# A gated long convolution with a routed feed-forward on one core: first filter block on ScalarE's DMA queue, keys and values as two pieces, another order of issue

## Chip, cores and metric

One core of a Trainium2 chip. The metric is the device time of one execution in microseconds (us), the median of several runs. A core has five engines with one instruction stream each: TensorE (PE in the profile, its weight loads PEld), VectorE (DVE), ScalarE (ACT), GpSimd (POOL) and SyncE (SP). Each works through its stream in order; an instruction that waits holds everything behind it on its engine. DMAs are issued by SP, by ACT or by POOL, and issuing one takes time on the issuing engine (SPq, ACTq, POOLq in the rows).

## What is computed

The input is 2048 tokens of 640 channels. The reference, cut to what matters:

```python
mod = (silu(c) @ w_mod)                 # six vectors sa, ca, ga, sb, cb, gb
h = layernorm(x) * (1 + ca) + sa
x = x + ga * A(h, k, v, shift_k, ssm_k, ssm_D)
h = layernorm(x) * (1 + cb) + sb
x = x + gb * B(h, w_r, w_gate, w_up, w_down)

def A(q, k, v, ...):
    kv = shift(k) * v                   # 4-tap causal convolution of k, per channel
    y  = irfft(rfft(kv) * rfft(ssm_k))  # causal convolution of length 2048, per channel
    return q * (y + kv * ssm_D)

def B(x, ...):                          # only the 8 tokens with the largest r = x @ w_r
    y = (silu(xs @ w_gate) * (xs @ w_up)) @ w_down * sigmoid(r[idx])
    return x + scatter_add(y at idx)
```

## The kernel before

The 640 channels are five blocks of 128, and each block goes through the same steps. The long convolution is a discrete Fourier transform in two steps, with the length 2048 split as 16 times 128, so that both steps are matrix products. Names of steps stand in the table `ORDER`, with the block's number behind them:

- `LK b` loads keys `kT` and values `vT` of block b, transposed by the DMA (`load_kv`, L129 and L130, on SP's queue). `LG b` loads the filter block `gA` (`load_g`, L140). `LX` loads a quarter of x into `xq` (L658).
- `C b` (`t_C`): PE forms the 4-tap convolution of `kT` with four diagonal matrices `dg` (`DIAG b`, L309) in two halves of 1024 tokens; each half is multiplied by `vT` into `kvT` (L80; in the starred form ACT copies the half first, L77, and DVE multiplies after it, L78), and written to DRAM as `kvd` (L373). `kvT` has a single buffer. `LXA b` reads `kvd` back in another layout as `xA` (L145).
- `G b` and `X b` (`stage_A`): the first step of the transform, of the filter and of the signal, four PSUM tiles each, copied out as `A`. Ahead of `G b` the skip weights `Dt` are added to the filter (L353).
- `BG b` and `BX b` (`stage_B`): the second step with the tables `FT`, four tiles each, copied out as `HX`. `P b` multiplies the two spectra on DVE (L406, L407, L409, L410).
- `BT b`: the first step back, with the tables `IT`; its tiles `U` go to DRAM (`UW`) and come back as `uA` (`LU`). `AT b` is the last step, multiplied by the normalised rows `h`, and `AA b` adds the result to `xq`.
- `Sx` are the statistics of the first layernorm (L664), `H` builds `h` from them and from the modulation vectors (`LW` loads, `MOD` computes). `R`, `GR`, `COL` and `GB` prepare the second layernorm and the scores.
- `T` is, in 11 parts, the choice of the 8 tokens, their feed-forward and the scattered addition to the output; `N`, `BS`, `BL` and `F` are the normalisation and the output rows of all tokens (16 halves `F`: a product L735 and a sum L737, then a DMA to the output). `WG` and `WD` load the feed-forward's weights.

Every copy out of PSUM goes to ACT or, where the name in `ORDER` ends in a star, to DVE (the class `Evac`). There are four PSUM tiles for these results, used in turn. PE, DVE and ACT all work in the order in which `ORDER` names the steps; `:n` means n parts of a step. Nothing else sets the order.

At the start, `SC`, `SA`, `SB`, `SD`, `SE`, `SG`, `SH` and `TC` make constants: POOL counts and compares (`trig` for the tables, `ident`, the mask `early` from `erow` and `ecol`, `arow`, `irow`, `onesb`), `TAB` turns `trig` into `FT` by sines on ACT, `RA` makes the matrix of `stage_A`, and `WU` runs 13 matmuls on zeros. `SG` sets `Dt` to zero on POOL (L236) and then loads the skip weights into it on SP's queue (L240). In `SA` ACT issues three small loads: `shk_bf` (the 4 taps, L201), `cT_bf` (L202) and `wr_c` (L203). `silu_c`, which the modulation starts from, needs `cT_bf`.

Of the kernel before, what the change touches and what calls it, by code (L numbers as in the profile page):

```python
# [9 lines left out]
P = 128  # L10
BF = mybir.dt.bfloat16
# [6 lines left out]
S_TOK = 2048  # L18
# [14 lines left out]


ORDER = """
SH SB0 LG0 SA TAB0 SC SE SG WU TAB0 RA SB1 SD TAB1 RAT RA LK0 G0 DIAG0 LG1 LX G0* LK1 C0 TAB1 DIAG1 G0* IT* G0
C0 BG0 LX TC BG0 G1 LXA0 Sx G1* Sx IT:2 C1:2 G1* LG2 G1 LXA1 BG0 BG0* LW BG1 Sx BG1* X0:3 X0* BG1 LK2 LX BX0 Sx
BX0:3 RAT Sx:2 DIAG3 Sx P0 BG1 X1* X1 G2 Sx DIAG2 LX X1 P0 X1 P0 LW C2:2 MOD G2 BX1:2 P0 G2 BX1 LW LXA2 G2 Sx
BT0:4 Sx P1 BG2 Sx:2 LW Sx:4 LK3 Sx BG2 LG3 P1 MOD BX1 LW MOD OG H LW X2:4 C3*:2 BG2 LW BX2 BG2 UW0 P1 BT1 BT1*
G3:2 H DIAG4 LXA3 MOD:2 LW P1 LK4 BX2* G3 UW1 H BX2:2 P2:2 BT1 H G3 MOD UW0 MOD BT1 P2 LW X3:2 LG4 X3 BG3 H C4*  # L40
X3 C4 H BT2 BG3 P2 BX3 BG3 H BX3 P3 BX3 WG BT2 UW1 WG LXA4 H P3 BT2 WG BT2 MOD BX3 BG3 G4*:2 G4 MOD P3 UW2 G4
X4:3 X4* BG4 P3 BG4* BX4 UW2 BX4 BG4 BX4 LU0 LU2 BG4 BX4 LU1 BT3:2 H P4:4 BT3 H:3 BT3 BT4:2 UW3 BT4 UW3 UW4 BT4
AT0*:2 AA0:2 AT1* COL UW4 LU3 AT1 R0 AA1:2 AT2* GB LU4 WG AA2 WG AT2* GR R0 WG AA2 WG R1 AT3 AT3* WG:2 R1 R2
AA3:2 AT4 AA4 GR AT4* R2 AA4 BS* R3 BS* GR R4 COL WD BL* R3 BS* GR:3 R4 T WD BS T N N* N:4 F BS WG T F BL F T N
F BS F T F N F:2 N:2 F N:2 F N BS F T N F N F N F BS F T F T:4
"""


# [14 lines left out]
def _kernel_body(ctx, tc, A_q, A_k, A_v, A_shift_k, A_ssm_k, A_ssm_D,  # L63
                 B_w_r, B_w_gate, B_w_up, B_w_down, c, w_mod, out):
    nc = tc.nc
# [22 lines left out]
    ring = ctx.enter_context(tc.tile_pool(name="ring", bufs=1))  # L88
# [35 lines left out]

    def load_kv(b):
        kT = ring.tile([P, 16 + S_TOK], BF, name="kT", tag="K", bufs=5)
        vT = ring.tile([P, S_TOK], BF, name="vT", tag="K", bufs=5)
        nc.gpsimd.memset(kT[:, 0:16], 0.0)
        nc.sync.dma_start_transpose(out=kT[:, 16:16 + S_TOK], in_=k_d[:, b * P:(b + 1) * P])  # L129
        nc.sync.dma_start_transpose(out=vT[:], in_=v_d[:, b * P:(b + 1) * P])  # L130
        kTs[b], vTs[b] = kT, vT

    def rows_ap(handle_ap, b, rowlen, run):

        return bass.AP(tensor=handle_ap.tensor, offset=handle_ap.offset + b * P * rowlen,
                       ap=[[run, P], [8 * rowlen, 16], [1, run]])
# [29 lines left out]
    cT_bf = const.tile([P, NB], BF, name="cT_bf")  # L166
    wr_c = const.tile([P, NB], BF, name="wr_c")
# [26 lines left out]
    def iota(o, pat, base=0, cm=0):  # L194
        nc.gpsimd.iota(o, pattern=pat, base=base, channel_multiplier=cm, allow_small_or_imprecise_dtypes=True)
# [3 lines left out]
    def t_SA():  # L199
        with nc.allow_non_contiguous_dma(reason="tiny transposed loads"):  # L200
            nc.scalar.dma_start(out=shk_bf[:], in_=A_shift_k.rearrange("(b p) j -> p b j", p=P))  # L201
            nc.scalar.dma_start(out=cT_bf[:], in_=c.rearrange("o (t p) -> p (o t)", p=P))  # L202
            nc.scalar.dma_start(out=wr_c[:], in_=B_w_r.rearrange("(t p) -> p t", p=P))  # L203
        for i, v in enumerate((PI, -PI, -math.pi / 2, -4096.0, -0.5)):
            G.memset(bias[:, i:i + 1], v)
        nc.scalar.activation(out=junk1[:], in_=bias[:, 2:3], func=ACT.Sin)
        iota(pidx[:], [[0, 1]], cm=1)
        yield
# [501 lines left out]
    tiny = lambda name, dt=F32: small.tile([P, M], dt, name=name)  # L710
# [207 lines left out]
@with_exitstack  # L918
def kernel(
    ctx: ExitStack,  # L920
    tc: tile.TileContext,
    A_q: bass.AP,
    A_k: bass.AP,
    A_v: bass.AP,
    A_shift_k: bass.AP,
    A_ssm_k: bass.AP,
    A_ssm_D: bass.AP,
    B_x: bass.AP,
    B_w_r: bass.AP,
    B_w_gate: bass.AP,  # L930
    B_w_up: bass.AP,
    B_w_down: bass.AP,
    c: bass.AP,
    w_mod: bass.AP,
    out: bass.AP,
):
    _kernel_body(ctx, tc, A_q, A_k, A_v, A_shift_k, A_ssm_k, A_ssm_D,
                 B_w_r, B_w_gate, B_w_up, B_w_down, c, w_mod, out)
# [30 lines left out]
```

## Time and profile before

| | |
|---|---|
| median of 3 runs | 172.56 us (171.92 to 173.59) |
| the profiled execution | 171.51 us, its span 169.7 us |
| PE, DVE, ACT, POOL busy in the span | 146.4, 145.1, 136.0, 35.7 us |
| DMA | 40.71 MB, 240 GB/s on average |

Times in the rows are us from the start of the span, of one execution. In a timeline a row gives start, duration, engine, line, operation, output and input, and in brackets the idle time before it and what ended it. A row of the waits gives who waited for what: us in total, times, the longest. In the table of windows each row is a stretch with its length and then the busy time and the number of instructions on PE, PEld, DVE, ACT and POOL, the granted clock of PE (1.00 is 2.4 GHz, 0.50 is 1.2 GHz), the DMA share and GB/s. A row of the chain gives start, duration and what. A row of groups gives line, operation, shapes, count, busy us and mean ns; a row of DMA issues gives the count, the size and the us to landing.

### The profile page before, as it was taken

To read this page: it belongs to the slowest core of one execution; us is meant where nothing else is said; L and a number is where in the kernel's file an instruction comes from. 1 tells how busy PE (TensorE), PEld (TensorE's weight loads), DVE (VectorE), ACT (ScalarE), POOL (GpSimd) and SP (SyncE) were. 2 spreads that over 40 slices of the span, in tenths; PEclk is the share of its full clock that TensorE was granted. 3 is DMA by queue.
4 is the path that set the end of the run, shared out by engine and by line. 5 is a ranking of instruction groups with operands and counts; after the bars stand their busy time and mean duration, and the time that the engine had idled before them with its cause. 6 is when DMAs were issued, how large, how long until landed. Compare 5 with 4: busy or idle time off the path is not lost.

```text
span 169.7 us, 4737 instructions
## 1 busy us (share of the span) xinstructions
PE 146.4 (86%) x1983; PEld 114.3 (67%) x1983; DVE 145.1 (85%) x265; ACT 136.0 (80%) x150; POOL 35.7 (21%) x78
## 2 busy tenths in 40 slices
PE   0869998988999999999999989999899883969850
PEld 0336856887488866898589869979788761257540
DVE  3667838899999929999999999999999998979940
ACT  3979694699889999989989999999498624999700
POOL 8838900060000062970000000000000102200003
PEclk9999999999999999999999999999999997595555
DMA  6299999999999999999999999997997369665640
GB/s 120 5 177 255 243 239 296 268 281 208 342 328 278 232 171 250 265 292 186 339 232 349 277 351 301 282 321 292 278 313 242 108 194 372 175 160 190 220 159 2
DMA packets 73405, 40.71 MB, mean 240 GB/s; under 512 B 45160, under 2 KB 70184, under 8 KB 73384
## 3 DMA queue, kind: packets, MB, share of 16 engines
q1 hardware_dynamic: 69560, 38.19, 88.0%
q10 hardware_dynamic: 3744, 2.22, 4.4%
q8 instruction: 15, 0.25, 0.7%
q0 software_dynamic: 80, 0.01, 0.1%
q14 instruction: 6, 0.05, 0.1%
HBM read 24.67 MB, written 10.50 MB: 207 GB/s over the span
## 4 chain that ended last, share of the span: by engine, by line
DVE 60%; DMA 12%; PE 10%; issue 6%; SPq 4%; POOL 3%; POOLq 1%; ACT 1%; DVEq 0%; ACTq 0%
DVE T L406 6%; DVE HX L407 5%; DVE A L58 5%; DMA kvd<-kvT 4%; DVE kvT L80 3%; DMA vT<-in_A_v_dram 3%; DVE st L664 3%; DMA kT<-in_A_k_dram 3%; DVE HX L410 3%; DVE HX L409 3%; DVE HX L58 3%; DVE xq L472 3%; DVE h L679 3%; DVE h L675 3%; PE p L367 2%
## 5 line engine op out<-in xcount | busy, mean ns | idle before, releaser
L60 ACT CAST HX<-ps 128x1024 bf16<-128x1024 f32 x28 | 27.8, 1045 | 3.5 <-PE ps L390 3.5
L386 PE MATMUL ps<-A,FT 128*128 128x256 bf16 x124 | 28.4, 273 | 0.4 <-DVE kvT L80 0.3
L388 PE MATMUL ps<-A,FT 128*128 128x128 bf16 x124 | 27.2, 219 | 0.0
L390 PE MATMUL ps<-A,FT 128*128 128x128 bf16 x124 | 27.2, 219 | 0.0
L60 ACT CAST A<-ps 128x1024 bf16<-128x1024 f32 x22 | 22.4, 1067 | 3.9 <-PE ps L346 3.9
L390 PEld LDWEIGHTS <-FT 128*128 128x128 bf16 x160 | 15.6, 98 | 1.8
L60 ACT CAST U<-ps 128x1024 bf16<-128x1024 f32 x16 | 16.2, 1079 | 0.5 <-ACT A L60 0.5
L386 PEld LDWEIGHTS <-FT 128*128 128x128 bf16 x160 | 15.6, 98 | 1.4 <-DVE A L58 0.9
L388 PEld LDWEIGHTS <-FT 128*128 128x128 bf16 x160 | 15.7, 98 | 1.2 <-issue 0.7
L424 PE MATMUL ps<-IT,HX 128*128 128x256 bf16 x68 | 15.4, 273 | 0.3 <-DVE HX L410 0.3
L422 PE MATMUL ps<-IT,HX 128*128 128x256 bf16 x68 | 15.4, 272 | 0.0
L367 PEld LDWEIGHTS <-dg 128*128 128x128 bf16 x80 | 7.7, 98 | 9.1 <-DVE dg L309 0.4
L664 DVE BATCH_NORM_STATS2 st<-xq 128x6 f32<-128x320 bf16 x32 | 13.3, 478 | 0.1
L309 POOL TENSOR_SCALAR dg<-ident,shk_f 128x128 bf16<-128x128 bf16 x16 | 12.6, 804 | 3.2 <-DVE shk_f L306 3.2
L407 DVE TENSOR_TENSOR HX<-HX 128x2048 bf16<-128x2048 bf16 x10 | 12.3, 1225 | 0.3
L406 DVE TENSOR_TENSOR T<-HX 128x2048 bf16<-128x2048 bf16 x10 | 12.2, 1216 | 0.0
L60 ACT COPY xT<-ps 128x2048 bf16<-128x2048 bf16 x4 | 7.5, 1865 | 3.8 <-PE ps L527 3.1
L353 POOL TENSOR_TENSOR gA<-gA,Dt 128x16 bf16<-128x16 bf16 x4 | 3.8, 942 | 30.4 <-DMA gA<-in_A_ssm_k_dram 15.9
L60 ACT CAST A<-p 128x1024 bf16<-128x1024 f32 x9 | 9.5, 1052 | 0.7 <-PE p L346 0.6
L367 PE MATMUL p<-kT,dg 128*128 128x512 bf16 x40 | 9.5, 379 | 0.4 <-DMA kT<-in_A_k_dram 0.3
L346 PEld LDWEIGHTS <-xA 128*128 128x128 bf16 x80 | 7.7, 97 | 3.0 <-issue 1.8
L346 PEld LDWEIGHTS <-gA 128*128 128x128 bf16 x80 | 7.5, 98 | 3.2 <-DVE shk_f L306 1.7
(259 smaller groups left out, 389.4 us busy)
## 6 DMA issues: line engine op xcount, KB each, us to landing
Ud<-U SPq DMA_DIRECT2D x10, 512.0 KB, 4.5
uA<-Ud SPq DMA_DIRECT2D x10, 512.0 KB, 7.0
gA<-in_A_ssm_k_dram SPq DMA_DIRECT2D x5, 512.0 KB, 5.3
xq<-in_A_q_dram SPq DMA_DIRECT2D x4, 640.0 KB, 5.2
kvd<-kvT SPq DMA_DIRECT2D x10, 256.0 KB, 3.3
xA<-kvd SPq DMA_DIRECT2D x5, 512.0 KB, 4.8
early<-in_w_mod_dram SPq DMA_DIRECT2D x3, 800.0 KB, 7.3
wm<-in_w_mod_dram SPq DMA_DIRECT2D x6, 400.0 KB, 6.2
```

The source lines that it names most:

```text
L58: self.nc.vector.tensor_copy(out=out, in_=in_)
L60: self.nc.scalar.copy(out=out, in_=in_)
L346: nc.tensor.matmul(ps[:, bb // 2, :, (bb % 2) * 8:(bb % 2) * 8 + 8], lhsT=src[:, 4 * g4 + bb, :], rhs=RA[:].rearrange("p k c e -> p (k c) ...
L367: nc.tensor.matmul(ps[:, i, :], lhsT=diags[b][:, j, :], rhs=kT[:, n0 - j:n0 - j + 512], start=(j == 0), stop=(j == 3))
L386: nc.tensor.matmul(ps[:, i], lhsT=FT[:, 0, k2, :], rhs=A[:, 2 * k2:2 * k2 + 2, u, :], start=True, stop=False)
L388: nc.tensor.matmul(ps[:, i, 0, :], lhsT=FT[:, 1, k2, :], rhs=A[:, 2 * k2 + 1, u, :], start=False, stop=False)
L390: nc.tensor.matmul(ps[:, i, 1, :], lhsT=FT[:, 2, k2, :], rhs=A[:, 2 * k2, u, :], start=False, stop=True)
L406: V.tensor_tensor(out=T2[:], in0=X, in1=Hi, op=ALU.mult)
L407: V.tensor_tensor(out=X, in0=X, in1=Hr, op=ALU.mult)
L422: nc.tensor.matmul(ps[:, i, :], lhsT=hx[:, k2, 0, 1, :], rhs=IT[:, k2, 1:3, :].rearrange("p a b -> p (a b)"), start=True, stop=False)
L424: nc.tensor.matmul(ps[:, i, :], lhsT=hx[:, k2, 1, 1, :], rhs=IT[:, k2, 0:2, :].rearrange("p a b -> p (a b)"), start=False, stop=True)
L664: V.bn_stats(out=st1[:, m, hf, :], in_=xq[:, m, hf * 320:hf * 320 + 320])
```

## The change

Three things are edited, and with them the whole table `ORDER`.

The filter of block 0 is loaded by ACT's queue in `SA`, behind `shk_bf`; the loads of `cT_bf` and `wr_c` leave `SA` and become a step `SY`, issued by SP. `load_kv` becomes a step of two parts, so that keys and values can stand at different places of the order.

```diff
     def load_kv(b):
         kT = ring.tile([P, 16 + S_TOK], BF, name="kT", tag="K", bufs=5)
-        vT = ring.tile([P, S_TOK], BF, name="vT", tag="K", bufs=5)
         nc.gpsimd.memset(kT[:, 0:16], 0.0)
         nc.sync.dma_start_transpose(out=kT[:, 16:16 + S_TOK], in_=k_d[:, b * P:(b + 1) * P])
+        yield
+        vT = ring.tile([P, S_TOK], BF, name="vT", tag="K", bufs=5)
         nc.sync.dma_start_transpose(out=vT[:], in_=v_d[:, b * P:(b + 1) * P])
         kTs[b], vTs[b] = kT, vT
+        yield
...
             nc.scalar.dma_start(out=shk_bf[:], in_=A_shift_k.rearrange("(b p) j -> p b j", p=P))
-            nc.scalar.dma_start(out=cT_bf[:], in_=c.rearrange("o (t p) -> p (o t)", p=P))
-            nc.scalar.dma_start(out=wr_c[:], in_=B_w_r.rearrange("(t p) -> p t", p=P))
+            load_g(0, nc.scalar)
...
+    def t_SY():
+        with nc.allow_non_contiguous_dma(reason="tiny transposed loads"):
+            nc.sync.dma_start(out=cT_bf[:], in_=c.rearrange("o (t p) -> p (o t)", p=P))
+            nc.sync.dma_start(out=wr_c[:], in_=B_w_r.rearrange("(t p) -> p t", p=P))
+        yield
...
-                  LK=lambda b: once(load_kv, b), LG=lambda b: once(load_g, b), LXA=lambda b: once(load_xA, b))
+                  LK=load_kv, LG=lambda b: once(load_g, b), LXA=lambda b: once(load_xA, b))
...
-SH SB0 LG0 SA TAB0 SC SE SG WU TAB0 RA SB1 SD TAB1 RAT RA LK0 G0 DIAG0 LG1 LX G0* LK1 C0 TAB1 DIAG1 G0* IT* G0
+SC SA SD SB0 RA SG LK0:2 WU TAB0:2 SB1 SE TAB1:2 LG1 RA LX DIAG0 G0*:4 LK1 C0:2 BG0:2 DIAG1 G1* G1 LK1 BG0 LXA0
```

On POOL the constants stand in another order: ahead of the memset of `Dt` there are now `pint`, the counter `early`, `bias`, `pidx`, `ident` and the first `trig`; `arow`, `irow` and `onesb` come much later, and the mask behind the second `trig`.

The start of SP's queue, in the kernel before:

```order
L140 DMA gA<-in_A_ssm_k_dram 128x16x128
L240 DMA Dt<-in_A_ssm_D_dram 8x80x1
L129 DMA_TRANSPOSE kT<-in_A_k_dram 128x2048
L130 DMA_TRANSPOSE vT<-in_A_v_dram 128x2048
L140 DMA gA<-in_A_ssm_k_dram 128x16x128
L658 DMA xq<-in_A_q_dram 128x4x640
L129 DMA_TRANSPOSE kT<-in_A_k_dram 128x2048
L130 DMA_TRANSPOSE vT<-in_A_v_dram 128x2048
L373 DMA kvd_238<-kvT 128x1024 x2
L658 DMA xq<-in_A_q_dram 128x4x640
L145 DMA xA<-kvd_238 128x16x128
```

The same stretch now (the first `kT` and `vT` are those of block 0, the second those of block 1):

```order
L247 DMA Dt<-in_A_ssm_D_dram 8x80x1
L128 DMA_TRANSPOSE kT<-in_A_k_dram 128x2048
L131 DMA_TRANSPOSE vT<-in_A_v_dram 128x2048
L142 DMA gA<-in_A_ssm_k_dram 128x16x128
L665 DMA xq<-in_A_q_dram 128x4x640
L128 DMA_TRANSPOSE kT<-in_A_k_dram 128x2048
L380 DMA kvd_241<-kvT 128x1024 x2
L131 DMA_TRANSPOSE vT<-in_A_v_dram 128x2048
L147 DMA xA<-kvd_241 128x16x128
L665 DMA xq<-in_A_q_dram 128x4x640
```

The write of block 0's product has moved ahead of block 1's values, and its reading back ahead of the second quarter of x; the first filter block is gone from this queue.

DVE's stream around block 3's product and the first products of `P`, in the kernel before:

```order
L409 TENSOR_TENSOR HX_461<-HX_461,T2_113 128x8x128
L410 TENSOR_TENSOR HX_461<-HX_461,T2_113 128x8x128
L592 TENSOR_TENSOR modv_101<-modv_101 128x640
L593 TENSOR_TENSOR modv_101<-modv_101 128x640
L675 TENSOR_SCALAR h_929<-xq_102,rs1_120,nm1_121 128x640 x4
L78 TENSOR_TENSOR kvT_960<-kvT_960,vT_850 128x1024 x2
L406 TENSOR_TENSOR T2_114<-HX_461 128x2048
```

And now, from the first half of that product to the second:

```order
L78 TENSOR_TENSOR kvT_927<-kvT_927,vT_855 128x1024
L416 TENSOR_TENSOR HX_382<-HX_382,T2_113 128x8x128
L417 TENSOR_TENSOR HX_382<-HX_382,T2_113 128x8x128
L413 TENSOR_TENSOR T2_114<-HX_382 128x2048
L414 TENSOR_TENSOR HX_382<-HX_382 128x16x128
L599 TENSOR_TENSOR modv_101<-modv_101 128x640
L600 TENSOR_TENSOR modv_101<-modv_101 128x640
L78 TENSOR_TENSOR kvT_927<-kvT_927,vT_855 128x1024
```

The two halves stood side by side; now six other instructions stand between them. Block 4's halves stood side by side too and are nine instructions apart now, a pair L413 and L414 (L406 and L407 before) among them as here.

Copies out of PSUM are shared out a little differently: all four of `G0` are on DVE now, two of the three `IT` copies instead of one; one `HX` copy moves from DVE to ACT. In the last part DVE forms five `base` sums of 1024 elements by itself instead of four, and ACT five instead of six. In the tail the first of the two `hT` products stands behind four more halves of `F` than before, and the second one further back by one half.

## Rows read from the trace of the kernel before

**Rows 1.** Windows: three stages, from the start to the end.

```profile
0.00:26.07 26.07, 19.39 (x142) 11.59 (x143) 15.27 (x33) 19.23 (x19) 16.67 (x54) 1.00 0.92 175
...
38.39:118.27 79.88, 78.05 (x784) 64.30 (x782) 75.97 (x108) 76.16 (x88) 11.96 (x9) 1.00 1.07 279
...
140.11:169.70 29.59, 18.45 (x320) 11.49 (x320) 21.05 (x63) 17.89 (x24) 3.82 (x8) 0.59 0.56 182
```

**Rows 2.** Waits, of the engines and of SP's queue.

```profile
DVE kvT L80 <- DMA kvd<-kvT: 3.5, 1, 3.5
...
DVE nm L668 <- POOL rs L667: 3.1, 1, 3.1
...
ACT modv L576 <- PE p L570: 1.6, 1, 1.6
...
SPq L240 <- POOL Dt L236: 4.9, 1, 4.9
```

**Rows 3.** Timeline of POOL, its first 8 us.

```profile
0.85 0.34 POOL L195 IOTA arow<- 128x128 f32 x1 [0.41 <-POOLq L953]
...
1.51 1.01 POOL L195 IOTA trig<- 128x1024 f32 x1
...
3.11 0.77 POOL L195 IOTA erow<- 128x128 f32 x1
...
5.95 0.16 POOL L236 MEMSET Dt<- 128x80 bf16 x1
...
7.04 0.20 POOL masks.py:197 MEMSET ident<- 128x128 bf16 x1
...
7.99 0.15 POOL L128 MEMSET kT<- 128x16 bf16 x2
```

**Rows 4.** Timeline of SP's queue to the first read back.

```profile
6.14 0.79 SPq L240 DMA_DIRECT2D Dt<-in_A_ssm_D_dram  x1
...
14.06 4.97 SPq L129 DMA_TRANSPOSE kT<-in_A_k_dram  x1
19.07 3.13 SPq L130 DMA_TRANSPOSE vT<-in_A_v_dram  x1
...
26.00 0.37 SPq L145 DMA_DIRECT2D xA<-kvd  x1
```

**Rows 5.** The chain that ended last, its two early DMAs.

```profile
6.99 5.50 DMA kT<-in_A_k_dram
...
22.92 3.03 DMA kvd<-kvT
```

**Rows 6.** DMA issues, the reading back of the products.

```profile
xA<-kvd SPq DMA_DIRECT2D x5, 512.0 KB, 4.8
```

**Rows 7.** Timeline of DVE, three places.

```profile
10.92 0.23 DVE L353 TENSOR_TENSOR gA<-gA,Dt 128x16 bf16<-128x16 bf16 x1 [1.07 <-DMA Dt<-in_A_ssm_D_dram]
...
38.39 1.20 DVE L406 TENSOR_TENSOR T<-HX 128x2048 bf16<-128x2048 bf16 x1
...
161.35 0.20 DVE L854 TENSOR_TENSOR hT<-gs,ps 128x48 bf16<-128x48 bf16 x1
```

**Rows 8.** Timeline of ACT: a small DMA issue, copies of `IT` and of `U`.

```profile
1.26 0.82 ACTq L202 DMA_DIRECT2D cT_bf<-in_c_dram  x1
...
21.55 3.67 ACT L60 COPY IT<-ps 128x2048 bf16<-128x2048 bf16 x2
...
55.31 2.04 ACT L60 CAST U<-ps 128x1024 bf16<-128x1024 f32 x2
```

**Rows 9.** Groups by shape on DVE: copies out of PSUM, sums for `base`.

```profile
L58 DVE CAST A<-ps 128x1024 bf16<-128x1024 f32 x7 | 8.5, 1219 | 0.8 <-PE ps L346 0.7
...
L497 DVE TENSOR_TENSOR base<-xq,modv 128x1024 bf16<-128x1024 bf16 x3 | 2.0, 683 | 0.0
```

**Rows 10.** Windows of 2 us around PE's pause in the tail.

```profile
140.00:142.00 2.00, 0.00 (x0) 0.00 (x0) 1.69 (x10) 0.90 (x1) 1.18 (x5) 1.00 1.06 385
142.00:144.00 2.00, 1.39 (x4) 0.52 (x5) 1.69 (x11) 0.91 (x2) 0.00 (x0) 0.56 1.07 364
```

More of the change, by code (lines that the diff above doesn't have):

```diff
@@ L35 @@
 ORDER = """
-SH SB0 LG0 SA TAB0 SC SE SG WU TAB0 RA SB1 SD TAB1 RAT RA LK0 G0 DIAG0 LG1 LX G0* LK1 C0 TAB1 DIAG1 G0* IT* G0
[L37 to L45, printed above, removed]
+SC SA SD SB0 RA SG LK0:2 WU TAB0:2 SB1 SE TAB1:2 LG1 RA LX DIAG0 G0*:4 LK1 C0:2 BG0:2 DIAG1 G1* G1 LK1 BG0 LXA0
+G1 IT Sx:3 G1* LX C1* C1 BG1* BG1 X0:2 SH X0 Sx LK2 Sx LG2 DIAG3 LXA1 LW Sx X0 IT* BG1* LK2 IT* BX0:2 BG1 P0 BG0
+BX0:2 SY LX G2 X1 P0 X1 Sx RAT X1 G2 X1 Sx LX DIAG2 P0 LW C2 BT0* C2 MOD G2 P0 LW G2 BX1 BT0:2 TC BX1 Sx:2 BT0
+Sx LK3 LXA2 LW BX1 Sx BG2 BX1 LK3 BG2 MOD Sx RAT LG3 BG2 Sx:3 UW0 P1 Sx C3* X2:2 P1 LK4 P1 MOD X2 LW X2 OG C3*
+DIAG4 MOD BX2 BG2 H G3 BT1 P1 BX2 LK4 LXA3 G3 LG4 G3 H BT1 P2 C4 H:2 G3 LW UW0 BX2 BT1 LW MOD BX2 P2 BT1 UW1 P2
+X3 LW X3 BG3 C4 X3 H X3 UW1 BT2 BG3 MOD BX3 P2 BX3 H MOD H BX3 WG BT2 H BX3 BG3 LXA4 BG3 WG P3 G4*:2 G4:2 H UW2
+WG BT2 P3 X4 LW MOD BT2 P3 BT3 X4 X4* X4 LU0 H BG4 BG4* UW2 BX4 P3 BX4 P4 BG4:2 BX4:2 MOD LU1 BT3:3 P4 BT4 P4
+BT4 P4 BT4 H:2 BT4 LU2 UW3 AT0 AA0 UW3 AT0* AA0 UW4 AT1* COL AT1* AA1:2 UW4 LU3 R0 AT2 LU4 AT2* WG GB R0 WG R1
+AA2:2 AT3 GR AT3* WG R1 WG AA3 R2 AA3 GR BS* AT4* COL AA4 AT4* AA4 BS* R3 R2 GR R4 WD BS*:3 GR:2 WD GR R3 R4 BL
+T N* WG T N:4 WG N:6 F BS N T F:2 WG BL T F BS F T F N F BS N F:4 N F:2 N F:2 T F T:5
 """
@@ L904, in run @@
             next(tasks[name])
-    MAKERS = dict(SA=t_SA, SB=t_SB, SC=t_SC, SD=t_SD, SE=t_SE, SG=t_SG, SH=t_SH, WU=t_WU, TC=t_TC, RA=lambda: short_tables(0), RAT=lambda: short_tables(2), DIAG=t_DIAG,
+    MAKERS = dict(SA=t_SA, SB=t_SB, SC=t_SC, SD=t_SD, SE=t_SE, SG=t_SG, SY=t_SY, SH=t_SH, WU=t_WU, TC=t_TC, RA=lambda: short_tables(0), RAT=lambda: short_tables(2), DIAG=t_DIAG,
                   TAB=t_TAB, IT=t_IT, G=t_G, X=t_X, C=t_C, BG=lambda b: stage_B(b, 0), BX=lambda b: stage_B(b, 1), P=t_P, BT=t_BT, LU=t_LU, UW=t_UW, AT=t_AT, AA=t_AA, F=t_F, N=t_N, BS=t_BS, BL=t_BL, T=t_T, GR=t_GR, R=t_R,
                   LW=t_LW, MOD=t_MOD, OG=t_OG, COL=t_COL, GB=t_GB, LX=t_LX, Sx=t_S1, H=t_H, WG=t_WG, WD=t_WD,
-                  LK=lambda b: once(load_kv, b), LG=lambda b: once(load_g, b), LXA=lambda b: once(load_xA, b))
+                  LK=load_kv, LG=lambda b: once(load_g, b), LXA=lambda b: once(load_xA, b))
     for item in ORDER.split():
```

## Prediction

> **What bounds the kernel now.** I read the windows by stage first. Up to 26.07 us DVE is busy 15.27 us and so idle 10.80 us, ACT 19.23; from 38.39 to 118.27 DVE is busy 75.97 of 79.88 us and ACT 76.16; in the tail DVE is busy 21.05 of 29.59 us [rows 1]. So in the long middle DVE and ACT are both full, each with not quite 4 us of idle time, and the time that can be had without taking work away lies in the first 26 us. The waits say where: SP's queue stands 4.9 us until POOL has set `Dt` to zero, and DVE stands 3.5 us until block 0's product has left the single `kvT`; the wait of 3.1 us for `rs` is in the middle and is not touched [rows 2]. The chain agrees: it runs over the landing of the first `kT` and over the first write `kvd` [rows 5].
>
> In the profiled execution the time is 171.51 us, 1.05 below the median of the runs shown. All terms come from that execution; I subtract their sum from the median as well.
>
> **Part 1: the skip weights and keys leave earlier.** POOL sets `Dt` at 5.95. Ahead of it stand the three constants from 0.85 to 1.51 (0.66 us) and the mask from 3.11 to 5.95 (2.84 us); both are behind it now. In their place comes `ident`, 7.04 to 7.99 (0.95 us) [rows 3]. 0.66 + 2.84 - 0.95 = 2.55 us. The load of `Dt` is issued near 3.6 instead of 6.14, and all behind it on SP's queue moves with it: `kT` of block 0 from 6.99 to 4.45, landing 5.50 us later at 9.95 [rows 4, 5], `kT` of block 1 from 14.06 to 11.5 [rows 4].
>
> That this lands earlier does not start PE 2.5 us earlier, because something else is late next: the mask now comes behind the second `trig`. 3.6 + 0.15 + 1.01 + 2.84 gives 7.6 us [rows 3]; behind it DVE has seven small instructions (two for `RA`, the taps, four diagonals), at L353's 0.23 us some 1.6 us, and then adds the skip weights, at 9.2 instead of 10.92 [rows 7]. So 1.7 of the 2.55 us reach `G0`.
>
> **Part 2: block 0's product goes out before block 1's values.** All four copies of `G0` and the two products of `C0` are on DVE, six instructions of 1.22 us [rows 9] (a product reads the same 1024 columns from PSUM): 9.7 + 6 x 1.22 = 17.0. SP is then done with the issue of block 1's keys, 11.5 + 4.97 = 16.5, so both writes go at 17 or before and land 3.03 us later, at 20.1 [rows 4, 5]. The values of block 1 take the queue meanwhile, 3.13 us, to 20.3 [rows 4]. The reading back `xA` follows at 20.4 instead of 26.00: 5.6 us earlier. DVE's wait for `kvT` goes; late next is `vT` of block 1, issued 1.9 us earlier than before, and about 1 us of the 3.5 comes back there.
>
> From this read to the first product of `P0` it is 26.00 to 38.39, 12.4 us [rows 4, 7], over a landing of 4.8 us [rows 6], `X0` and `BX0`. I keep that length: 32.8. Counted in the two orders, DVE has done about the same work by then (two copies more, a pair of statistics and a table less), so DVE can be 5.6 us ahead. Its idle time ahead of that point, over 11 us, leaves room.
>
> **Part 3: ACT has not done as much.** At that point ACT has one copy of `IT` (3.67 / 2 = 1.84 us) and two copies of 1.02 us fewer behind it [rows 8], 3.9 us in all. In the stage that follows it was idle 79.88 - 76.16 = 3.7 us [rows 1], so at DVE's pace it would have no idle time at all. Of the 3.7, 1.6 is the wait for the first modulation matmul [rows 2], which stands behind the same table load in both orders; the rest are waits for PE. The ends are that all of it stays (3.7 us held back) or none. I take 2.4: the 1.6 and somewhat over a third of the rest. 5.6 - 2.4 = 3.2 us gained, ends 1.9 and 5.6.
>
> **Part 4: the small edits.** `gA` of block 0 on ACT's queue costs nothing: its sum waits for `Dt` and the mask in any case. The two tiny loads leave ACT's start, where an issue took 0.82 us [rows 8], and stand on SP behind the third `vT`: at most 1.6 us there, covered by the 5 us by which SP is ahead, and lost if it is not. DVE forms one `base` sum more, 0.68 us [rows 9], in a stage where it has no idle time: a loss of 0.7. In the tail the second `hT` (161.35 [rows 7]) stands one half of `F` later; by columns (1280 to 1024) that is 0.85 us, an estimate from rows 9. The scattered addition also waits for the last output row, which leaves no later, so I take 0.2, ends 0 and 0.85.
>
> **Sum.** 3.2 - 0.7 - 0.2 = 2.3 us. 171.51 - 2.3 = 169.2 for a profiled execution, 172.56 - 2.3 = 170.3 for the median.
>
> **Rivals.** *All of the front stays.* ACT closes its waits, since PE is ahead as well: 5.6 - 0.9 = 4.7 us, 167.9. For it: ACT has 0.9 us less to do over the whole stage. Against it: one engine at 95% may close its gaps, two that wait for the same four PSUM tiles seldom do.
>
> *The gain is eaten.* PE works in order, and in the second block the filter load now stands behind a transposing load on SP. If `G2` and `X1` come 2 us late, or if PE's clock falls at the start, 172.3 to 172.6 remains. On the clock the rows show this: PE does nothing from 140 to 142 and is granted 0.56 in the 2 us behind it, between the two levels of 1.2 and 2.4 GHz [rows 10]. In the changed kernel PE pauses about 1.5 us between the warm-up matmuls and `G0`, and again while DVE alone copies `G0`. If it falls there, some 4 us of matmuls take 8, and I take half as hidden below the copies: 2 us. The Trainium skill, "TensorE: Matmul & The Clock Gate", Part 1, says that a slow clock is the default and that activity releases it; by it, a thinner start speaks against this order. Rows 10 agree for the longer pause; no row here shows a fall after a short one.
>
> *Slower.* From the second half of a product to the landing of its `xA` it is 3.03 + 0.37 + 4.8 = 8.2 us [rows 4 to 6], and PE stands in order at `X3` and `X4` if they come first. In the order now, the halves of blocks 3 and 4 are no longer side by side: an L406 and an L407 stand in each gap, 2.4 us with the 1.20 of the one row for both [rows 7]. If nothing covers that, twice 2.4 = 4.8 us are lost: 172.56 - 2.3 + 4.8 = 175.1. It decides from a loss of 4.0 us. For it: the middle has no slack. Against it: SP is ahead, and blocks 3 and 4 are issued earlier than they were.
>
> **How the numbers follow.** A measurement here tells about 1% from no change, that is 170.8 and 174.3. The forecast has a chance of 0.45 (169.5 to 171.6, with 1.6 to 3.7 us held back by ACT), all but 0.05 of it below 170.8; the larger gain 0.17; the eaten gain 0.22; slower 0.16. That gives faster 0.57, same 0.27, slower 0.16. The range leaves out the best of the larger gain and the worst of the slower case: 166.8 to 175.0.
>
> **What would show it.** In the profile of the changed kernel: `Dt`'s load issued near 3.6; `xA` read near 20.4; `P0`'s first product near 33; no wait of DVE for `kvd` in the first 30 us; ACT with under 3 us of idle time from there to the last `U`. Part 1 is wrong if `G0` starts at 11 as before, part 2 if `xA` is not read before 24, part 3 if ACT's copies end 5 us earlier or not earlier at all. If PE's granted clock is under 1.00 ahead of 20 us, or if PE stands at `X3` or `X4`, the rivals hold. The whole is wrong if DVE's idle time in the middle grows by 4 us or more.

## The result, and the profile after

The changed kernel takes 174.09 us (median of 22 runs) where the kernel before, on the same chip, takes 172.62 (22 runs). The ratio is 1.0061, 95% interval 1.0035 to 1.0087: some 1.1 us slower, where 2.3 us faster was forecast. The ratio leaves out the seven executions that took over 1.5% longer than the changed kernel's fastest (172.69), and the profiled one is among them (177.03 us, its span 175.3). So what lies behind 60 us is also read from e4 below, whose instructions are the same up to the first `AT` and whose span is 171.8.

The front of the program does what was forecast. SP's queue in the changed kernel, answering to [rows 4] and to the `Dt` wait of [rows 2]:

```profile
3.33 0.81 SPq L247 DMA_DIRECT2D Dt<-in_A_ssm_D_dram  x1
4.19 3.02 SPq L128 DMA_TRANSPOSE kT<-in_A_k_dram  x1
...
17.28 4.02 SPq L131 DMA_TRANSPOSE vT<-in_A_v_dram  x1
21.85 0.37 SPq L147 DMA_DIRECT2D xA<-kvd  x1
```

DVE's timeline, answering to [rows 7]:

```profile
9.07 0.22 DVE L360 TENSOR_TENSOR gA<-gA,Dt 128x16 bf16<-128x16 bf16 x1
...
34.00 1.23 DVE L413 TENSOR_TENSOR T<-HX 128x2048 bf16<-128x2048 bf16 x1
```

`Dt` leaves at 3.33 (forecast 3.6), the skip weights are added at 9.07 (9.2), block 0's product is read back at 21.85 (20.4; 26.00 before), and the first product of `P0` starts at 34.00 (32.8; 38.39 before). Windows of the changed kernel, the first and the second of them beside [rows 1]:

```profile
0.00:26.07 26.07, 21.00 (x154) 13.07 (x155) 20.58 (x35) 18.46 (x19) 12.39 (x37) 1.00 1.00 194
38.39:118.27 79.88, 74.85 (x695) 59.45 (x692) 69.58 (x105) 70.60 (x83) 16.24 (x30) 0.96 1.02 260
...
0.00:34.00 34.00, 28.46 (x249) 19.85 (x250) 26.80 (x45) 24.69 (x25) 12.39 (x37) 1.00 1.03 209
0.00:60.00 60.00, 53.25 (x479) 38.70 (x480) 50.84 (x91) 48.35 (x53) 25.16 (x61) 1.00 1.03 231
60.00:80.00 20.00, 16.07 (x139) 12.12 (x138) 14.33 (x20) 16.73 (x19) 4.96 (x7) 0.95 1.21 233
```

And of the kernel before, to the same three points:

```profile
0.00:38.39 38.39, 30.66 (x272) 21.45 (x273) 26.78 (x50) 28.42 (x29) 19.26 (x60) 1.00 1.00 209
0.00:60.00 60.00, 51.56 (x466) 37.99 (x467) 48.08 (x88) 48.37 (x52) 19.26 (x60) 1.00 1.01 233
60.00:80.00 20.00, 19.84 (x183) 15.66 (x182) 16.80 (x24) 19.09 (x24) 11.59 (x8) 1.00 1.20 237
```

Read the columns DVE, ACT and GB/s. By its first `P0` product DVE has worked 26.80 us in the one and 26.78 in the other, so in busy time it is 4.4 us ahead. (0.75 us of the 26.80 is no lead: one `trig` instruction took 1.63 us instead of 0.88.) ACT has worked 24.69 us by then instead of 28.42. By 60 us DVE has worked 2.8 us more than before, ACT nothing more (48.35 to 48.37), and the transfers are not ahead either: 231 GB/s over 60 us is 13.9 MB, 233 is 14.0. From 60 to 80 us the lead shrinks: DVE does 2.5 us of work less than before and ACT 2.4, and in e4 0.8 and 1.4:

```profile
60.00:80.00 20.00, 17.87 (x161) 13.98 (x161) 16.04 (x24) 17.72 (x21) 5.43 (x8) 1.00 1.20 242
```

That is one row of e4's windows. What they wait for there (waits of the changed kernel in the middle, in the columns of [rows 2]):

```profile
ACT modv L583 <- PE p L577: 3.7, 1, 3.7
...
PE p L577 <- DVE kvT L80: 3.3, 1, 3.3
DVE nm L675 <- POOL rs L674: 3.1, 1, 3.1
...
DVE kvT L78 <- DMA vT<-in_A_v_dram: 2.7, 1, 2.7
...
DVE kvT L80 <- DMA vT<-in_A_v_dram: 1.2, 1, 1.2
```

Only the wait for `rs` was there before. (ACT's wait of 1.6 us for a matmul in [rows 2] is another one, and stands in both kernels.) DVE waits for the values of blocks 3 and 4. The first half of block 4's product, which ACT copied out of PSUM before and DVE now takes from there itself, is late by that; the PSUM tile is not free, PE stands 3.3 us before a modulation matmul, and ACT stands behind PE. In e4 the three are 2.2 (`vT`), 2.1 (PE) and 1.7 us (ACT). Where the values are late by, on SP's queue, first the changed kernel:

```profile
47.59 7.43 SPq L128 DMA_TRANSPOSE kT<-in_A_k_dram  x1
55.12 0.52 SPq L147 DMA_DIRECT2D xA<-kvd  x1
...
57.25 3.80 SPq L131 DMA_TRANSPOSE vT<-in_A_v_dram  x1
...
65.75 2.96 SPq L128 DMA_TRANSPOSE kT<-in_A_k_dram  x1
...
70.37 0.32 SPq L380 DMA_DIRECT2D kvd<-kvT  x1
70.80 2.70 SPq L131 DMA_TRANSPOSE vT<-in_A_v_dram  x1
```

and the kernel before:

```profile
52.21 0.37 SPq L145 DMA_DIRECT2D xA<-kvd  x1
...
55.24 2.91 SPq L129 DMA_TRANSPOSE kT<-in_A_k_dram  x1
58.25 2.24 SPq L130 DMA_TRANSPOSE vT<-in_A_v_dram  x1
...
74.23 4.67 SPq L129 DMA_TRANSPOSE kT<-in_A_k_dram  x1
78.96 2.06 SPq L130 DMA_TRANSPOSE vT<-in_A_v_dram  x1
```

The keys of block 3 are issued 7.7 us earlier, but the issue alone holds the queue for 7.43 us instead of 2.91, and the values behind it leave only 1.0 us earlier. DVE, however, is ready for them 4.9 us earlier: at 62.0 (64.65 less the wait) instead of 66.95. First the changed kernel, then the kernel before:

```profile
64.65 0.69 DVE L78 TENSOR_TENSOR kvT<-kvT,vT 128x1024 bf16<-128x1024 bf16 x1 [2.65 <-DMA vT<-in_A_v_dram]
```

```profile
66.95 1.29 DVE L78 TENSOR_TENSOR kvT<-kvT,vT 128x1024 bf16<-128x1024 bf16 x2
```

Block 4's keys leave 8.5 us earlier than before and its values 8.2, but the new order needs them earlier by about as much: its first half is formed at 77.95 instead of 85.88, after a wait of 1.2 us. SP reaches these values only behind the write of block 3's second half (70.37), so the delay of block 3 is handed on to block 4.

The chain that ended last says the same. Of the changed kernel, in its second profile (e9):

```profile
47.46 7.72 SPq L128
...
57.42 7.22 DMA vT<-in_A_v_dram
70.92 7.16 DMA vT<-in_A_v_dram
```

and of the kernel before, further down the chain of [rows 5]:

```profile
55.24 2.91 SPq L129
...
58.25 5.81 DMA vT<-in_A_v_dram
```

Before, the chain already ran over block 3's keys and values. Now it runs over them for longer, and over block 4's values as well. Block 3's values land at 64.6 (57.42 and 7.22) where they landed at 64.1 before (58.25 and 5.81).

The tail from `msq` on takes 29.8 us instead of 29.6: the 0.2 of part 4.

### The profile page after: what moved, and what is told of

The parts are those of the page before. It is cut to its first block, busy times and chain, and to the rows that moved or that the text cites. A ratio compares the mean times of both kernels' runs of the same rounds, so it can differ in the third digit from the quotient of the medians.

```text
span 175.3 us, 4720 instructions
## 1 busy us (share of the span) xinstructions
PE 147.7 (84%) x1979; PEld 115.0 (66%) x1979; DVE 147.2 (84%) x266; ACT 134.6 (77%) x149; POOL 35.3 (20%) x78
## 2 busy tenths in 40 slices
DMA packets 73405, 40.71 MB, mean 232 GB/s; under 512 B 45160, under 2 KB 70184, under 8 KB 73384
## 4 chain that ended last, share of the span: by engine, by line
DVE 41%; PE 18%; DMA 16%; ACT 7%; SPq 6%; issue 5%; POOL 4%; POOLq 1%; DVEq 0%; ACTq 0%
DMA vT<-in_A_v_dram 8%; DVE A L58 4%; SPq L128 4%; DMA xq<-in_A_q_dram 4%; ACT A L60 3%; DMA kvd<-kvT 3%; DVE T L413 3%; PE ps L393 3%; DVE HX L414 2%; DVE kvT L80 2%; PE ps L468 2%; DVE HX L417 2%; DVE IT L742 2%; DVE FT L744 2%; DVE FT L742 2%
## 5 line engine op out<-in xcount | busy, mean ns | idle before, releaser
L60 ACT CAST HX<-ps 128x1024 bf16<-128x1024 f32 x26 | 26.3, 1048 | 5.2 <-PE ps L397 5.0
L397 PE MATMUL ps<-A,FT 128*128 128x128 bf16 x116 | 25.8, 222 | 0.0
L395 PE MATMUL ps<-A,FT 128*128 128x128 bf16 x116 | 25.8, 222 | 0.0
L60 ACT CAST A<-ps 128x1024 bf16<-128x1024 f32 x25 | 24.8, 1038 | 1.1 <-PE ps L353 1.1
L60 ACT CAST U<-ps 128x1024 bf16<-128x1024 f32 x15 | 15.1, 1041 | 0.9 <-PE ps L431 0.7
L431 PE MATMUL ps<-IT,HX 128*128 128x256 bf16 x60 | 14.5, 283 | 0.2 <-DVE HX L417 0.2
L429 PE MATMUL ps<-IT,HX 128*128 128x256 bf16 x60 | 14.4, 282 | 0.0
L374 PE MATMUL ps<-kT,dg 128*128 128x512 bf16 x56 | 13.1, 379 | 0.3 <-ACT A L60 0.3
L60 ACT CAST HX<-p 128x1024 bf16<-128x1024 f32 x11 | 11.5, 1046 | 1.9 <-PE p L397 1.8
L414 DVE TENSOR_TENSOR HX<-HX 128x2048 bf16<-128x2048 bf16 x10 | 12.2, 1225 | 0.3
L413 DVE TENSOR_TENSOR T<-HX 128x2048 bf16<-128x2048 bf16 x10 | 12.2, 1216 | 0.3 <-ACT HX L60 0.3
L353 PE MATMUL ps<-RA,gA 128*128 128x256 bf16 x68 | 9.5, 273 | 2.5 <-DVE gA L360 1.9
L316 POOL TENSOR_SCALAR dg<-ident,shk_f 128x128 bf16<-128x128 bf16 x16 | 10.6, 673 | 0.5 <-DVE shk_f L313 0.5
L393 PE MATMUL p<-A,FT 128*128 128x256 bf16 x44 | 10.3, 272 | 0.4 <-DVE IT L58 0.4
```

The lines of the kernel that those rows point to most:

```text
L60: self.nc.scalar.copy(out=out, in_=in_)
L316: (V if b == 0 else nc.gpsimd).tensor_scalar(out=dg[:, j, :], in0=ident[:], scalar1=shk_f[:, b, j:j + 1], scalar2=None, op0=ALU.mult)
L353: nc.tensor.matmul(ps[:, bb // 2, :, (bb % 2) * 8:(bb % 2) * 8 + 8], lhsT=src[:, 4 * g4 + bb, :], rhs=RA[:].rearrange("p k c e -> p (k c) ...
L374: nc.tensor.matmul(ps[:, i, :], lhsT=diags[b][:, j, :], rhs=kT[:, n0 - j:n0 - j + 512], start=(j == 0), stop=(j == 3))
L413: V.tensor_tensor(out=T2[:], in0=X, in1=Hi, op=ALU.mult)
L414: V.tensor_tensor(out=X, in0=X, in1=Hr, op=ALU.mult)
```

## The experiments

Theory D: the transfers are not ahead as the engines are, and so the lead is waited away at blocks 3 and 4. Rivals: PE is the bound (P); the last stage's order loses the time; the front's gain was never there. Most of these kernels cut the two orders apart: one order up to a step, and the other's order for all that is left. All ratios are to the kernel before on the same chip, with their 95% intervals; the last columns are single profiles, and the four kernels with the whole order of before or nearly so (before, e6, e15, e18) have `msq` between 140.1 and 142.5, which is how far one profile can be trusted there. e3, e4, e10 and e12 have four runs each, e8 six; for e3, e4, e8 and e10 this leaves the verdict unclear. The profiled runs of e4 (173.61 us) and e10 (172.29) are the fastest of their four, so their last columns are better than their ratios.

| run | ratio | first `P0` | last `P4` product | `msq` |
|---|---|---|---|---|
| before | 1 | 38.4 | 109.9 | 140.1 |
| changed (e9: 1.0103, 1.0047 to 1.0159) | 1.0061 (1.0035 to 1.0087) | 34.0 | 114.6 (e9: 113.5) | 145.5 (e9: 144.6) |
| e1 front alone | 0.9965 (0.9922 to 1.0009) | 37.6 | 110.2 | 141.4 |
| e2 rest alone | 1.0094 (1.0063 to 1.0126) | 38.9 | 111.8 | 144.1 |
| e12 last stage alone | 1.0123 (1.0093 to 1.0154) | 38.5 | 110.4 | 144.0 |
| e4 last stage of before | 1.0146 (1.0074 to 1.0218) | 33.9 | 110.2 | 142.3 |
| e3 `vT3`, `vT4` early | 1.0165 (1.0096 to 1.0235) | 33.6 | 114.2 | 145.8 |
| e10 weights behind block 3 | 1.0190 (1.0129 to 1.0251) | 33.3 | 110.0 | 140.9 |
| e5 fifth of the weights | 0.9942 (0.9902 to 0.9981) | 33.3 | 107.7 | 139.0 |
| e6 the same, before | 0.9995 (0.9959 to 1.0031) | 38.7 | 110.3 | 141.1 |
| e13 e5, last stage of before | 0.9892 (0.9852 to 0.9933) | 34.8 | 109.0 | 140.2 |
| e16 `C4` copied by ACT | 1.0026 (0.9986 to 1.0066) | 34.0 | 111.2 | 142.6 |

**The parts of the order.** e1 and e2 cut at the first `P0`, e4 and e12 at the first `AT`.

First e1, from the changed kernel:

```diff
-IT* BG1* LK2 IT* BX0:2 BG1 P0 BG0 BX0:2 SY LX G2 X1 P0 X1
+IT* BG1* LK2 IT* BX0:2 BG1 SY RAT TC BG0* LX BX0:2 RAT Sx P0 X1* X1
```

and e2, from the kernel before:

```diff
-BX0:3 RAT Sx:2 DIAG3 Sx P0 BG1 X1* X1 G2 Sx DIAG2
+BX0:3 RAT Sx:2 DIAG3 Sx BG1 P0 G2 X1 P0 X1:2 G2 X1
```

> The changed kernel's order up to the first half of P0 of block 0, then the kernel before's order for all that is left. Theory (the front brings about 4.4 us, and what comes behind it in the changed order loses it): 4.4 us below the kernel before, 167.5 to 169.5, with DVE's first product of P0 near 34 and the whole middle that much earlier. Rival (the front's gain dies at once, at PE, POOL or G2, whatever order follows): within 1.5 us of the kernel before, 171 to 174.

> The kernel before's order up to P0, then the changed kernel's order for all that is left (the first filter block still on ScalarE's queue). Theory: it has the losses of the middle and of the stage behind it without the front's gain, so about 5 us above the kernel before, 176 to 179. Rival (front and rest are each worth nothing): 172 to 174.

e1 brings 0.6 us (0 lies within its interval), not 4.4, so its time is the rival's. In it `P0` starts only 0.8 us earlier than before: the copy, the table and the statistics that the changed order puts behind `P0` stand ahead of it again. By 34.00 e1 and the changed kernel have done the same work on DVE and ACT; in the 3.6 us from there to `P0` DVE is busy 3.2 us and ACT 3.1. e2 is slower by 1.6 us, between its two expectations. That is no more than the last stage costs alone (e12 below, 2.1), so behind the old start the changed middle by itself shows no loss.

e4 from the changed kernel:

```diff
-LU2 UW3 AT0 AA0 UW3 AT0* AA0 UW4 AT1* COL AT1* AA1:2
+LU2 UW3:2 UW4 AT0*:2 AA0:2 AT1* COL UW4 LU3 AT1 R0 AA1:2
```

and e12 from the kernel before:

```diff
-AT0*:2 AA0:2 AT1* COL UW4 LU3 AT1 R0 AA1:2 AT2*
+AT0 AA0 AT0* AA0 AT1* COL AT1* AA1:2 UW4 LU3 R0 AT2
```

> The changed kernel up to the first AT, then the kernel before's order for all that is left. Theory: the stage from the end of U and h to msq takes 21.9 us again in place of 24.2, so 2.3 us below the changed kernel, near 171.8. Rival (this stage is longer only because it starts in another state, such as PE's clock or late transfers): no difference, 173.5 to 174.7.

> The kernel before's order up to the first AT, then the changed kernel's order for the rest. If that order costs 2.3 us by itself: 2 to 3 us above the kernel before, 174.7 to 175.7. If the stage only gives back what arrives early: within 0.8 us of the kernel before.

The two contradict each other. The changed last stage behind an unchanged start costs 2.1 us (e12); the unchanged one behind the changed start gives nothing back (e4). Both have four runs only. Where e12 stands, DVE's timeline:

```profile
141.56 0.69 DVE L493 TENSOR_TENSOR T<-pg,m 128x512 f32<-128x512 f32 x1 [0.97 <-PE pg L489]
...
143.74 0.20 DVE L548 TENSOR_TENSOR rsum<-rsum,pq 128x48 f32<-128x48 f32 x1 [0.66 <-PE pq L544]
```

DVE waits twice for PE's small matmuls, which now come later in PE's stream, where before it waited 0.27 us once.

**Transfers.** e3 puts the values of blocks 3 and 4 behind their keys again; e10 puts 800 KB of modulation weights behind block 3's transfers.

First e3:

```diff
-Sx LK3 LXA2 LW BX1 Sx BG2 BX1 LK3 BG2
+Sx LK3:2 LXA2 LW BX1 Sx BG2 BX1 BG2
...
-P1 LK4 P1 MOD X2 LW X2 OG C3* DIAG4 MOD BX2 BG2 H G3 BT1 P1 BX2 LK4 LXA3
+P1 LK4:2 P1 MOD X2 LW X2 OG C3* DIAG4 MOD BX2 BG2 H G3 BT1 P1 BX2 LXA3
```

and e10:

```diff
-G2 P0 LW G2 BX1 BT0:2 TC BX1 Sx:2 BT0 Sx LK3 LXA2 LW BX1 Sx BG2 BX1 LK3 BG2 MOD
+G2 P0 G2 BX1 BT0:2 TC BX1 Sx:2 BT0 Sx LK3 LXA2 LK3 LW BX1 Sx BG2 BX1 LW BG2 MOD
```

> The changed kernel with the values of blocks 3 and 4 loaded directly behind their keys again (two words of the order moved). Theory: DVE's waits for vT in C3 and C4 (2.7 and 1.2 us) and PE's pause of 3.3 us behind C4 with the half clock after it go, 2 to 4 us below the changed kernel: 170 to 172. Rival (the middle is bound by something else, or xA2 and kvd3, now behind a long issue on SyncE's queue, are late instead): 173.5 to 175.

> The changed kernel with the third piece of the modulation weights (800 KB) behind the keys, the product and the values of block 3 on SyncE's queue, and these values directly behind the product's read; the same bytes in all. Theory D: the keys of block 3 issue in 3 to 4 us in place of over 7, DVE's wait for vT there goes, 1.5 to 2.5 us below the changed kernel, 171.2 to 172.2. Rival (the lack is of bytes per time in all, so that any order has something late): the wait moves to the modulation weights or to xA, within 1 us of the changed kernel.

In place the rivals held: the wait moves. In time both ratios lie above all that was expected. In e3, between 60 and 80 us, it is for the reading back of block 2's product; in e10 for the weights that were put behind. The waits of e3:

```profile
PEld L353 <- DMA xA<-kvd: 4.3, 1, 4.3
ACT A L60 <- PE ps L353: 3.8, 1, 3.8
```

and of e10:

```profile
PEld L577 <- DMA early<-in_w_mod_dram: 3.5, 1, 3.5
```

So neither of these two places was the lack. For e10 this rests on the ratio of e11 below, which has the same middle and eight runs; e10's profile is of a run as fast as the kernel before, and why its other runs take 174.7 to 176.4 us is open. e5 and e6 take bytes away and leave every engine's work as it is:

```diff
-nc.sync.dma_start(out=wms[a], in_=wm[:, :, a * D:(a + 1) * D])
+nc.sync.dma_start(out=wms[a][:, 0:1, :], in_=wm[:, 0:1, a * D:(a + 1) * D])
...
-rhs=w[:, t, :], start=(t == 0),
+rhs=w[:, 0, :], start=(t == 0),
```

> The changed kernel with one fifth of the modulation weights loaded (one row block of five, read five times by the same matmuls; the modulation values are others). It takes some 3.7 MB of transfers away and no work of an engine. Theory D (from 40 to 65 us the transfers set the pace of blocks 2 and 3, so that the front's lead cannot be carried on): 2.5 to 4 us below the changed kernel, 170 to 171.5. Theory P (TensorE, some 97% busy in the middle, is the bound): within 1 us of the changed kernel.

> The kernel before with the same fifth of the modulation weights loaded. Theory D: the transfers of before are in step with its later start, so within 1 us of the kernel before, and e5 ends below it. Theory P: within 1 us of the kernel before as well, and e5 ends above it by the same 1 us as with all the weights.

This is the pair that decides. The changed kernel gains 1.2% (from 1.0061 to 0.9942), some 2.05 us, and is then faster than the kernel before; the kernel before gains nothing. No wait of DVE for `vT` is left in e5's middle. In e5 the keys of block 3 issue in 2.89 us at the same place of the queue, and the values leave 5.2 us earlier than in the changed kernel. SP's queue in e5:

```profile
46.84 2.89 SPq L128 DMA_TRANSPOSE kT<-in_A_k_dram  x1
49.84 0.52 SPq L147 DMA_DIRECT2D xA<-kvd  x1
...
52.06 2.44 SPq L131 DMA_TRANSPOSE vT<-in_A_v_dram  x1
```

Its windows, to be read beside those above:

```profile
0.00:60.00 60.00, 54.01 (x486) 39.59 (x487) 50.83 (x91) 48.88 (x53) 25.64 (x61) 1.00 1.02 221
60.00:80.00 20.00, 19.60 (x178) 15.16 (x176) 18.80 (x27) 19.65 (x24) 7.75 (x9) 1.00 0.84 196
```

From 60 to 80 us DVE and ACT do 2.8 and 1.9 us of work more than in e4, and the last product of `P4` is 2.2 us earlier than before: with the transfers relieved, ACT gets ahead of the kernel before as well, by 0.5 us at 60 us and 1.1 at 80. What the pair does not tell apart is the bytes and the time that SP's queue is held: fewer bytes shorten both. The Trainium skill, "DMA: Bandwidth & Descriptors", Specifications, wants at least 512 bytes per transfer for full rate; here 45160 of 73405 packets are smaller, and no run varied their size.

e14 and e15 use the first 5 us, in which the DMA engines are half idle (their share is 0.53 in the changed kernel), for the first 800 KB of these weights, with all bytes in place.

Here e14:

```diff
-SC SA SD SB0 RA SG LK0:2 WU
+LW SC SA SD SB0 RA SG LK0:2 WU
...
-LXA1 LW Sx X0 IT*
+LXA1 Sx X0 IT*
```

> The changed kernel with the first piece of the modulation weights (800 KB) issued first of all on SyncE's queue, where the DMA engines are half idle for 5 us, in place of at 33 us; all bytes as before. Theory D (bytes per time set the pace from 40 to 65 us): block 3's keys issue and land 1 to 3 us earlier, the waits for vT and for the PSUM tile shrink, 1.5 to 2.5 us below the changed kernel, 171.5 to 172.5. Rival (what matters is the order close to block 3, or the keys of block 0 now land late): within 1 us of the changed kernel, or above it.

> The kernel before with the same move. Theory D: its transfers keep up with its engines, so within 0.8 us of the kernel before. Rival (early bytes help any order): 1 us or more below it.

The ratios are 1.0088 (1.0039 to 1.0136) and 0.9980 (0.9946 to 1.0013): the rival for e14. The keys of block 3 issue in 5.64 instead of 7.43 us, but block 0's product is read back at 23.94 instead of 21.85: so what the middle gains the front may pay back, which is not shown (in this profile PE's granted clock also fell in the front, to 0.50 from 11 to 13 us).

**PE.** One tap of the convolution is left out: four matmuls of 512 columns per block (the 16 in the text below is a slip).

```diff
-for j in range(4):
+for j in range(3):
...
-start=(j == 0), stop=(j == 3))
+start=(j == 0), stop=(j == 2))
```

> The changed kernel with three of the four taps of the short convolution (the fourth left out): 16 matmuls of 512 columns fewer per half pair, about 0.85 us of TensorE per block, 3.4 us behind block 0, and no other engine's work. Theory P: 2.5 to 3.5 us below the changed kernel, near 171. Theory D, or a bound by VectorE and ScalarE together: within 1 us of the changed kernel.

> The kernel before with three of the four taps. Theory P: 2.5 to 3.5 us below the kernel before, near 170. Bound by VectorE and ScalarE together: within 1 us of the kernel before.

1.0091 (1.0051 to 1.0130) and 1.0111 (1.0016 to 1.0206): neither kernel gains (for e8 the verdict is unclear), although PE is busy 78.05 of 79.88 us in the middle [rows 1]; the six runs of e8 reach from 171.9 to 177.8 us, which no theory here explains. Theory P falls.

**The changed kernel again, the last stage behind relieved transfers, and the copy of `C4`.**

> The changed kernel as it is, beside the kernel before on the same chip. All theories: 0.4 to 0.9% above the kernel before. Theory D (the transfers set the pace of block 3): keys of block 3 take over 6 us to issue behind 800 KB of modulation weights, DVE waits about 2 us for vT of block 3 and PE about 2 to 3 us for the PSUM tile of block 4's product, in this profile too, without any fall of PE's clock.

1.0103, above the 0.4 to 0.9% expected though these lie within its interval, with the waits as expected (2.8 us for `vT`, 3.5 for the PSUM tile); but PE's clock did fall behind the pause. e11 is e10 with the last stage of before, e13 is e5 with it; the cut is that of e4.

> The same, and from the first AT on the kernel before's order. If the order of the last stage costs the changed kernel its 2.3 us by itself, 1.5 to 2.5 us below e10 and so 2 us or more below the kernel before; if that stage gives back whatever lead reaches it (PE is behind, and the transfers of U set its start), within 1 us of e10.

> e5 (changed kernel, a fifth of the modulation weights loaded) with the kernel before's order from the first AT on. If the order of the last stage costs by itself: 1.5 to 2.5 us below e5, 169 to 170. If that stage gives back what arrives early because the transfers of U or TensorE set its pace: within 0.8 us of e5.

e11: 1.0100 (1.0055 to 1.0146), 0.9% below e10, with intervals that overlap, and not below the kernel before. e13: 0.9892, 0.5% or 0.9 us below e5, with intervals that overlap, between its two expectations. e16 gives the copy of block 4's first half back to ACT, e17 does so with the last stage of before.

```diff
-BT1 P2 C4 H:2 G3 LW UW0
+BT1 P2 C4* H:2 G3 LW UW0
```

> The changed kernel with the first half of block 4's product copied out of PSUM by ScalarE, as in the kernel before (one star in the order). Theory (PE stands because DVE, late by vT, holds the fourth PSUM tile; the pause costs 2 us and, where the clock falls behind it, 3 more): PE's pause at the modulation matmul goes, no fall of the clock behind 60 us, 1.5 to 3 us below the changed kernel, 171.5 to 172.8, and a narrower spread. Rival (the transfers hold this stage back anyway, and the loss moves to the next wait): within 1 us of the changed kernel.

> The same with the kernel before's order from the first AT on. Theory (that order costs the changed kernel 2.1 us by itself, e12): 1.5 to 2.5 us below e16, 169.5 to 171, so below both kernels. Rival (the last stage gives back what arrives early, as e4 looked): within 0.8 us of e16.

e16: PE's pause and the fall of the clock are gone, yet the time is only 0.35% below the changed kernel's, and intervals overlap; DVE still waits 3.7 us for `vT`. The narrower spread did come: its twelve runs lie between 172.8 and 175.0 us, those of the changed kernel between 172.7 and 177.9. So the pause may be what spreads the changed kernel's runs; that is not shown. e17: 1.0006 (0.9965 to 1.0047), no faster than the kernel before, and so not the version that beats both.

**Part 2 alone**, in the kernel before, with `load_kv` in two parts:

```diff
-LG1 LX G0* LK1 C0 TAB1 DIAG1 G0* IT* G0 C0 BG0
+LG1 LX G0* LK1 C0 TAB1 DIAG1 G0* IT* G0 C0 LK1 BG0
```

> The kernel before with one thing changed: the values of block 1 are loaded behind the writes of block 0's product in place of ahead of them. By the prediction's part 2: the product is read back some 3 us earlier than 26.00, DVE's wait of 3.5 us for kvT shrinks and about 1 us of it comes back as a wait for vT, so 1 to 2.5 us below the kernel before, 170.2 to 171.7. By theory D (the transfers set the pace behind it): P0 is earlier by 1 us or more, the last P4 product is not, and the time is within 0.8 us of the kernel before.

0.9960 (0.9924 to 0.9996), 0.7 us. The read back is at 24.46 instead of 26.00, but DVE's wait for `kvd` of 3.5 us is replaced by one of 3.4 us for the values of block 1 (waits of e18), and `P0` starts at 38.4 as before, which neither text expected:

```profile
DVE kvT L80 <- DMA vT<-in_A_v_dram: 3.4, 1, 3.4
```

Where the 0.7 us come from is open. Among the kernels that load everything, e18 and e1 are the fastest measured, by 0.7 and 0.6 us.

## Why the prediction was wrong

- **Part 1: right.** Every time within 0.3 us.
- **Part 2: right in place, a size off.** `P0` came 4.4 us earlier, not 5.6: the read back at 21.85 instead of 20.4 (the write ahead of it took 4.90 us to land and not 3.03), and the wait for block 1's values is 1.7 us in the changed kernel instead of "about 1 us". By itself the part brings the wait back whole (e18).
- **Part 3: the count right.** ACT's 3.9 us of work left over were 3.7. "I take 2.4" of it as held back: in the changed kernel all of it was by 60 us, ACT being level with before. With transfers relieved and the order of before from the first `AT` on (e13), the front and middle are worth 1.9 us, where 3.2 was forecast: 1.3 too much. Of this, 1.2 is part 2's lead, 4.4 and not 5.6. What is held back there, 4.4 less 1.9, is near the 2.4. This is the smaller error.
- **The step that failed** is a cover: "covered by the 5 us by which SP is ahead", and in the slower rival "SP is ahead, and blocks 3 and 4 are issued earlier than they were". Issued earlier they were; ahead of the need they were not. By 60 us the two kernels have moved the same bytes, and block 2's read back leaves 2.9 us later. Block 3's values leave 1.0 us earlier and land some 0.5 us later, where DVE is ready 4.9 us earlier. The chain of the kernel before could have told: the prediction took from it the two early transfers [rows 5] and passed over block 3's keys and values, on which it runs later. The term was priced at 0 and measures 2.05 us (e5 against the changed kernel, with e6 as control).
- **Part 4.** The last stage was put at 0.7 us and the tail at 0.2. From e5 to e13, which differ in both, they measure 0.9 together (intervals overlap); behind the old start 2.1 (e12); from e16 to e17 0.35, within the error. Their size is not settled. The tail alone, from `msq` on, took the 0.2 more.
- **Sum by these terms:** 1.9 us gained, 0.9 lost behind the first `AT`, 2.05 lost to transfers: 1.05 us slower, as measured. Either error alone, 1.3 or 2.05, would have left a gain. This is a chain of single changes (e13, e5, changed kernel) and so adds up by itself; that its first link is the front's worth rests on e13's interval of 0.4%.
- **The rivals.** "The gain is eaten" comes nearest, by another mechanism than the two named: PE waits at most 0.8 us for the inputs of `G2` and `X1` in the changed kernel, and its granted clock is 1.00 up to 34 us. The slower rival saw that the halves of blocks 3 and 4 stand apart, but PE stood at the modulation matmul for a PSUM tile, not at `X3` or `X4`; e16 puts that at 0.35%, with intervals that overlap.
- **The signs.** `Dt`, `xA`, `P0` and the missing wait for `kvd` came as said. That the whole is wrong was to show in 4 us more of idle time of DVE in the middle: from 38.39 to 118.27 it was 3.9 us before and is 10.3 in the changed kernel's profile, 7.3 in e4.

## What to carry to other kernels

Ahead of a forecast that engines will run earlier, count the bytes moved by a fixed time in both: a lead that the transfers do not share ends at the next block whose inputs they bring. If moving one load only moves the wait to another, take bytes away in a control pair, on the kernel before and the one after; that helps to tell a lack of place from a lack of rate. And when several engines share the work, the lead that counts is that of the one that is least ahead.

## What the runs showed that was not expected

A transposing load of the same 512 KB held SP's queue for 2.89 us (e5), 2.91 (before), 5.64 (e14) or 7.43 us (changed kernel), by what was queued around it; e5 and the changed kernel differ in the bytes of the modulation weights alone.

PE's granted clock can fall from 2.4 to 1.2 GHz behind a pause in mid-kernel, as it does in the tail of [rows 10], but not always. Windows of the changed kernel, where PE stands until 79.2:

```profile
76.00:78.00 2.00, 0.00 (x0) 0.00 (x0) 0.83 (x2) 1.02 (x2) 0.00 (x0) 1.00 1.17 202
78.00:80.00 2.00, 0.78 (x4) 0.42 (x4) 2.00 (x2) 0.00 (x0) 0.00 (x0) 0.53 1.22 230
80.00:82.00 2.00, 2.00 (x13) 1.50 (x12) 2.00 (x6) 0.42 (x1) 0.00 (x0) 0.50 0.99 225
```

and of e7, whose pause at the same place is 3.2 us:

```profile
76.00:78.00 2.00, 0.00 (x0) 0.00 (x0) 1.97 (x3) 1.04 (x2) 0.00 (x0) 1.00 1.24 237
78.00:80.00 2.00, 1.32 (x14) 1.09 (x14) 2.00 (x3) 0.43 (x1) 0.00 (x0) 1.00 1.36 218
```

At the start, a pause of 2.1 us behind the warm-up matmuls was followed by 0.50 in e13, one of 1.5 us by 1.00 in e9. How much of the ratio such falls make up was not measured.
